# Attention with a wide feed-forward on one core: row maxima of two heads by one instruction, and scores that pass through a double and a single PSUM bank in turn

## The chip, the cores and the metric

The kernel runs on 1 core of one Trainium2 chip. The time is device microseconds of one execution; the figure for a kernel is the median of its runs. PE is TensorE (PEld its weight loads), DVE is VectorE, ACT is ScalarE, POOL is GpSimd, SP is SyncE. PSUM has eight banks here, each 512 float32 wide in 128 partitions, and which of them a step may write is what this case is about.

## The reference

One transformer block on x of 2048 rows by 576 columns: attention of 32 heads of 18 columns each with a full softmax, then a gated feed-forward of width 4608.

```python
x = A_x
h = x + _A_ref(_layernorm(x, axis=-1), A_wqkv, A_wo)
h2 = h + _B_ref(_layernorm(h, axis=-1), B_w_gate, B_w_up, B_w_down)

def _A_ref(x, wqkv, wo):                # H = 32, Dh = 18
    qkv = (lambda x, *d: x.transpose(*d))((x @ wqkv).reshape(B, S, 3, H, Dh), 2, 0, 3, 1, 4)
    q, k, v = qkv[0], qkv[1], qkv[2]
    scores = jnp.einsum("bhqd,bhkd->bhqk", q, k) * Dh ** -0.5
    p = _softmax(scores, axis=-1)
    o = jnp.einsum("bhqk,bhkd->bhqd", p, v)
    return (lambda x, *d: x.transpose(*d))(o, 0, 2, 1, 3).reshape(B, S, D) @ wo

def _B_ref(x, w_gate, w_up, w_down):
    g = jnp.einsum("bsd,df->bsf", x, w_gate)
    u = jnp.einsum("bsd,df->bsf", x, w_up)
    return jnp.einsum("bsf,fd->bsd", _gelu(g) * u, w_down)
```

## The kernel before, in words

Products are made in float16 with each operand split into a high and a low half, so one product of 576 columns is 14 matmuls into one bank (`accumulate`). The program has these stages.

1. Normalization of x, and the products that give q, k and v. The q and k halves go to DRAM (`qk_hi`, `qk_lo`) and come back as stacks of 54 rows for four heads at a time (`load_stacks`); in each stack two heads lie in rows 0 to 53 and 64 to 117.
2. Attention. The work is cut into NS = 32 blocks, indexed n: 8 groups of four heads times 4 blocks of 512 queries. A block has 16 steps, kt, one for each 128 keys. Softmax needs the row maxima first, so the scores are made twice.
   - Maxima (`max_unit`, L420 and L423): queries in the partitions, 512 keys along the row. A unit takes two heads: two matmuls, and the row maximum by DVE. A block has 32 such units, and they run 56 units (28 steps) ahead of the block that uses them. `max_finish` puts the maxima of a block together, PE turns them (L438) and they become two more rows of the q stack.
   - Scores (`scores_pair`, L461 and L463): keys in the partitions, 512 queries along the row, two heads into a double bank, and one Exp by ACT over 1024 elements into `pes`.
   - Weighing (`weigh`, L467): four float32 matmuls of 32 columns each, with v and a column of ones, add one step into the accumulator bank; in the trace they are eight rows.
   - After the 16th step `out_block` copies the accumulator (L476), turns it by four transposes (L480), divides on DVE (L483, L485) and stores on POOL.
   From step 484 on there are no maxima left to make.
3. During the last three blocks of attention, `wo_block` makes the output projection and the second normalization of the query blocks that are done (`fill`), and `split_gate_up` prepares the first feed-forward weights (`side`). The last `wo_block(3)` comes after attention.
4. Feed-forward: nine chunks of 512 columns, `gate_up` and `down`, with the next chunk's weights split beside them. `split_down` first needs the largest weight of the chunk: DVE reduces it (L122, L125), PE turns it (L129).

PE's order in stages 1 to 3 up to the end of attention is the order of the code, since it is scheduled by hand there. After it, and on the other engines, a scheduler decides, within what the buffers allow.

The eight PSUM banks before: two double banks `pair0` and `pair1` (`pair_ring`, for scores; their four halves are `single_ring`, for `gate_up`), and four single banks. The first three are `m_ring`: maxima, the two kinds of transposes, the products of `wo_block`, the small transposes of weights. The fourth, `singles[3]`, is the accumulator. `down` uses the four.

One step of the main loop before is: one unit of maxima, scores of the pair 0, scores of the pair 1, one unit of maxima, weighing of the step before.

## Time and profile before

| What | Value |
|---|---|
| Median of 3 runs | 2922.98 us (2922.92 to 2926.84) |
| The profiled execution | 2924.51 us, of which the span from first to last instruction 2922.7 us |
| PE, DVE, ACT busy over the span | 95%, 68%, 49% |
| Attention, from the first to the last weighing | 228.9 to 1591.2 us |
| Mean granted TensorE clock | 0.997 |

Times in the profile are microseconds from the start of the span. A row of the timeline has the start, the duration, the engine, the line, the operation, out<-in and a count; instructions that follow one another in one engine and line are merged into one row. In brackets stands idle time just before, and what ended it. A mean duration counts an instruction from its start to its end; the next one of the same engine may start before that end, so the distance between two starts is shorter than the duration.

### The profile page before, as it was taken

The numbers are of one execution on the slowest core, as the hardware profiler recorded it, in microseconds if no ns is written. First come the engines' busy times: TensorE is split into PE (matmuls) and PEld (weight loads), VectorE is DVE, ScalarE is ACT, GpSimd is POOL, SyncE is SP. The second block draws the span as 40 slices with busy tenths as digits, with TensorE's granted clock in tenths as the row PEclk, the third lists the DMA queues.
The fourth block names the chain that finished last, engine by engine and source line by source line (L and its number), as shares of the span: only waits on it lengthen the run. The fifth ranks groups of instructions, "written<-read, shape, count | busy, mean of one in ns | idle before, by whom it ended". The sixth has DMA issues, their size and how long they took to land.

```text
span 2922.7 us, 42983 instructions
## 1 busy us (share of the span) xinstructions
PE 2772.1 (95%) x17312; PEld 1168.1 (40%) x17312; DVE 1977.2 (68%) x3675; ACT 1440.0 (49%) x1684; POOL 100.4 (3%) x205
## 2 busy tenths in 40 slices
PE   6999899999999999999989999999999999999999
PEld 3532222222222222222233555555555555555555
DVE  7569999999999999999975725252525252524222
ACT  5217888888888888888757312121212121212111
POOL 0001000100001010100000000000000000000000
PEclk9999999999999999999999999999999999999999
DMA  8121000000000000000225301010101010100001
GB/s 224 51 74 53 1 25 1 26 1 10 17 1 25 1 26 1 25 5 1 58 56 122 105 1 53 1 53 1 53 1 53 1 53 1 53 1 1 1 17 50
DMA packets 105432, 95.13 MB, mean 33 GB/s; under 512 B 65872, under 2 KB 79312, under 8 KB 105232
## 3 DMA queue, kind: packets, MB, share of 16 engines
q1 hardware_dynamic: 100256, 83.81, 10.3%
q0 software_dynamic: 4976, 8.56, 1.0%
q8 instruction: 136, 2.23, 0.3%
q14 instruction: 64, 0.52, 0.1%
HBM read 63.70 MB, written 14.16 MB: 27 GB/s over the span
## 4 chain that ended last, share of the span: by engine, by line
PE 44%; ACT 3%; DVE 2%; DMA 1%; issue 1%; POOL 0%; ACTq 0%; SPq 0%
PE pair L267 27%; PE bank L267 15%; ACT WK L463 1%; DVE mx L423 1%; ACT W L238 1%; ACT V L238 1%; PE bank L467 1%; ACT V L598 0%; DMA X<-nat 0%; PE pair L461 0%; ACT W L598 0%; DMA X<-V 0%; DMA V<-in_B_w_down_dram 0%; ACT ga L613 0%; PE bank L420 0%
## 5 line engine op out<-in xcount | busy, mean ns | idle before, releaser
L423 DVE TENSOR_REDUCE mx<-bank 128x1 f32<-128x512 f32 x2048 | 1282.2, 683 | 61.4 <-PE bank L420 58.8
L463 ACT ACTIVATE WK<-pair,p_ex_sc 128x1024 f32<-128x1024 f32 x1024 | 1085.0, 1113 | 261.9 <-PE pair L461 261.7
L467 PE MATMUL bank<-WK,V 128*32 128x512 f32 x4096 | 548.7, 607 | 0.1
L267 PE MATMUL pair<-X,V 128*128 128x512 f16 x2240 | 489.0, 379 | 3.1 <-ACT ga L613 3.1
L267 PE MATMUL pair<-X,W 128*128 128x512 f16 x2128 | 469.0, 379 | 1.5 <-ACT ga L613 1.5
L615 DVE SCALAR_TENSOR_TENSOR ga<-pair,p_hsc,ga 128x512 f32<-128x512 f32 x144 | 107.8, 749 | 502.5 <-PE pair L267 502.5
L267 PEld LDWEIGHTS <-WK 128*128 128x128 f16 x3456 | 338.2, 98 | 93.2
L613 ACT ACTIVATE ga<-pair,p_gsc 128x512 f32<-128x512 f32 x144 | 98.8, 686 | 491.6 <-PE pair L267 491.6
L420 PE MATMUL bank<-W 54*128 54x512 f16 x1024 | 288.4, 382 | 54.3 <-DVE mx L423 18.1
L267 PEld LDWEIGHTS <-W 128*128 128x128 f16 x2296 | 222.5, 98 | 271.9 <-issue 16.3
L420 PE MATMUL bank<-A 54*128 54x512 f16 x1024 | 279.8, 383 | 46.7 <-DVE mx L423 12.0
L267 PEld LDWEIGHTS <-V 128*128 128x128 f16 x2240 | 218.5, 98 | 261.8 <-issue 3.9
L616 ACT CAST WK<-ga 128x512 f16<-128x512 f32 x144 | 89.0, 618 | 443.6 <-DVE ga L615 443.6
L634 DVE SCALAR_TENSOR_TENSOR nat<-bank,p_dsc,nat 128x288 f32<-128x288 f32 x288 | 148.0, 516 | 194.8 <-PE bank L267 194.8
L467 PEld LDWEIGHTS bank<-WK,V 128*32 128x32 f32 x4096 | 81.2, 108 | 409.2 <-issue 380.5
L267 PE MATMUL bank<-V,WK 128*128 128x288 f16 x1920 | 239.0, 286 | 0.0
L267 PE MATMUL bank<-W,WK 128*128 128x288 f16 x1536 | 191.4, 286 | 0.0
L461 PE MATMUL pair<-W 56*128 56x512 f16 x1024 | 161.1, 378 | 5.6 <-ACT WK L463 5.4
L420 PEld LDWEIGHTS <-W 54*128 54x128 f16 x1024 | 61.6, 93 | 242.2 <-issue 235.2
L461 PE MATMUL pair<-A 56*128 56x512 f16 x1024 | 157.1, 379 | 1.1 <-ACT WK L463 1.1
L420 PEld LDWEIGHTS <-A 54*128 54x128 f16 x1024 | 60.3, 93 | 231.4 <-issue 225.1
L617 DVE TENSOR_TENSOR WK<-ga,WK 128x512 f16<-128x512 f32 x144 | 99.3, 690 | 76.3 <-ACT WK L616 76.2
(154 smaller groups left out, 1140.9 us busy)
## 6 DMA issues: line engine op xcount, KB each, us to landing
V<-in_B_w_down_dram SPq DMA_DIRECT2D x9, 1152.0 KB
A<-in_B_w_gate_dram SPq DMA_DIRECT2D x9, 1024.0 KB
A<-in_B_w_up_dram SPq DMA_DIRECT2D x9, 1024.0 KB
qk_hi<-qk SPq DMA_DIRECT2D x36, 128.0 KB
qk_lo<-qk SPq DMA_DIRECT2D x36, 128.0 KB
A<-in_A_x_dram SPq DMA_DIRECT2D x32, 144.0 KB
out_dram<-nat SPq DMA_DIRECT2D x16, 288.0 KB
WK<-in_A_wqkv_dram SPq DMA_DIRECT2D x3, 1152.0 KB
```

Of the source, the lines that this page charges most:

```text
L238: nc.scalar.activation(wh[:, c], wf[:, c], AF.Copy, scale=sc)
L267: nc.tensor.matmul(dst, a, b, start=(i == 0), stop=(i == len(pairs) - 1))
L420: nc.tensor.matmul(pms[j][:, :TB], Q[r, q0 : q0 + P], K[r, kc * TB : (kc + 1) * TB], start=True, stop=True)
L423: nc.vector.tensor_reduce(mx[:, t, 2 * pr + j, kc : kc + 1], pms[j][:, :TB], axis=AX.X, op=ALU.max)
L461: nc.tensor.matmul(pS[:, j, :TB], K[r, kt * P : (kt + 1) * P], Q[r, qc * TB : (qc + 1) * TB], start=True, stop=True)
L463: nc.scalar.activation(pes[(2 * kt + pr) % NPE], pS[:, :, :TB], AF.Exp, scale=ex_sc)
L467: nc.tensor.matmul(acc[32 * hh : 32 * hh + 32, :TB], Vg[n // NB][:, kt * G4 + hh * VC : kt * G4 + hh * VC + 32], pes[(2 * kt + hh // 2) % ...
L613: nc.scalar.activation(ga, pg[:, :TB], AF.Gelu_apprx_tanh, scale=gsc)
L615: nc.vector.scalar_tensor_tensor(ga, pu[:, :TB], hsc, ga, op0=ALU.mult, op1=ALU.mult)
L616: nc.scalar.copy(hh[:, f], ga)
L617: nc.vector.tensor_sub(hl[:, f], ga, hh[:, f])
L634: nc.vector.scalar_tensor_tensor(nat[:, t, ws], pt[:, :HALF], dsc, nat[:, t, ws], op0=ALU.mult, op1=ALU.add)
```

## The change

PSUM is dealt out anew. Both double banks `max_pairs` now belong to the maxima: a unit's two matmuls go into the two halves of one, and one DVE instruction reduces 128x2x512 to 128x2. The scores have a double bank `sc_pair` and a single bank `sc_one`, and go through them in turn: two heads by an Exp of 1024 elements (`P`), one head by an Exp of 512 elements (`s`). As a step has four heads and P and s together three, the order of the units repeats every three steps. It is written as strings, with A for a unit of maxima and W for the weighing. `pes` has nine slots of one head each. The transposes of the maxima and of `out_block`, the products of `wo_block` and the small transposes of weights now use the halves of `max_pairs`, as `gate_up` does; the products of stage 1 and `down` use the other four banks. `wo_block` is begun at kt 5 instead of kt 1, and its two products in a step stand together behind the weighing.

```diff
-    pairs2 = [ps.tile([P, 2, 512], F32, name=f"pair{i}") for i in range(2)]
-    singles = [ps.tile([P, 512], F32, name=f"bank{i}") for i in range(4)]
+    max_pairs = [ps.tile([P, 2, 512], F32, name=f"pair{i}") for i in range(2)]
+    sc_pair = ps.tile([P, 2, 512], F32, name="scp")
+    sc_one = ps.tile([P, 512], F32, name="sco")
+    acc = ps.tile([P, 512], F32, name="acc")
...
-    pair_ring = ring(pairs2)
-    single_ring = ring([p[:, i] for i in range(2) for p in pairs2])
-    m_ring = ring(singles[:3])
-    down_ring = ring(singles)
+    pair_ring = ring(max_pairs)
+    m_ring = ring([p[:, i] for i in range(2) for p in max_pairs])
+    single_ring = m_ring
+    side_ring = ring([sc_pair[:, 0], sc_one, sc_pair[:, 1], acc])
+    down_ring = side_ring
...
-            pms = [next(m_ring) for j in range(2)]
+            pm = next(pair_ring)
...
-            for j in range(2):
-                nc.vector.tensor_reduce(mx[:, t, 2 * pr + j, kc : kc + 1], pms[j][:, :TB],
-                                        axis=AX.X, op=ALU.max)
+            nc.vector.tensor_reduce(mx[:, t, 2 * pr : 2 * pr + 2, kc], pm[:, :, :TB],
+                                    axis=AX.X, op=ALU.max)
...
+    NPE = 9
...
+    def scores(k):
+        h = done["h"]
+        if h + k > 4 * NS * NT:
+            return
+        done["h"] += k
+        dst = sc_pair if k == 2 else sc_one.unsqueeze(1)
...
+        nc.scalar.activation(pes[:, h % NPE : h % NPE + k], dst[:, :, :TB], AF.Exp, scale=ex_sc)
...
+        order = "APAsW", "PAAsPAsW", "PAsW"
+        for q in range(NS * NT + 1):
+            n, kt = divmod(q, NT)
+            for unit in order[q % 3][:-1]:
+                if unit == "A":
+                    take(mxs)
+                else:
+                    scores(2 if unit == "P" else 1)
+            take(side, 2)
+            if q > 0:
+                weigh(*divmod(q - 1, NT))
...
+            if q > 0:
+                take(fill, 2)
...
+            if n > NS - NB and kt == 5:
+                fill = wo_block(n % NB - 1)
```

How PE's queue changes, at three places. Weight loads and rows that repeat the one above are left out.

The first is a step in the middle of attention. Before, one step (L420 maxima into `bank0` to `bank2`, L461 scores, L467 weighing into `bank3`):

```order
L420 MATMUL bank1_69<-W_75 128x512
L420 MATMUL bank2_70<-W_75 128x512
L461 MATMUL pair0_66<-A_77 128x512
L461 MATMUL pair1_67<-A_77 128x512
L420 MATMUL bank0_68<-W_75 128x512
L420 MATMUL bank1_69<-W_75 128x512
L467 MATMUL bank3_71<-WK_76,V_73 32x512 x4
```

Now, the step of the string PAAsPAsW (L424 maxima, two matmuls to a row, L473 scores, `scp` the double and `sco` the single bank, L479 weighing):

```order
L473 MATMUL scp_68<-A_76 128x512
L424 MATMUL pair0_66<-W_74 128x512
L424 MATMUL pair1_67<-W_74 128x512
L473 MATMUL sco_69<-A_76 128x512
L473 MATMUL scp_68<-A_76 128x512
L424 MATMUL pair0_66<-W_74 128x512
L473 MATMUL sco_69<-A_76 128x512
L479 MATMUL acc_70<-WK_75,V_72 32x512 x4
```

Each head of the maxima had a bank of three in turn; now a unit of two heads has one double bank of two, and the scores one double and one single.

The second is the turning of a finished block, on PE, before (L480):

```order
L420 MATMUL bank0_68<-W_75 128x512
L420 MATMUL bank1_69<-W_75 128x512
L467 MATMUL bank3_71<-WK_76,V_73 32x512 x4
L480 MATMUL bank2_70<-id32_78,WK_76 128x128 x4
L420 MATMUL bank0_68<-W_75 128x512
```

and now (L491):

```order
L424 MATMUL pair1_67<-W_74 128x512
L473 MATMUL sco_69<-A_76 128x512
L479 MATMUL acc_70<-WK_75,V_72 32x512 x4
L491 MATMUL pair1_67<-id32_77,WK_75 128x128 x4
L473 MATMUL scp_68<-A_76 128x512
```

The transposes took the third bank, whose turn it was; now they write into half of the double bank that the unit of maxima just ahead of the weighing has filled.

The third is the end of attention, on PE. Before (X,V are the first products of `gate_up`, W,X the products of `wo_block(3)`, and L129 turns the largest weights: `am_gu` of the second chunk's gate and up, `am_dn` of the first chunk's down):

```order
L480 MATMUL bank0_68<-id32_78,WK_76 128x128 x4
L267 MATMUL pair0_66<-X_74,V_73 128x512
L267 MATMUL pair1_67<-X_74,V_73 128x512
L267 MATMUL bank1_69<-W_75,X_74 128x288
L267 MATMUL bank2_70<-W_75,X_74 128x288
...
L267 MATMUL pair1_67<-X_74,V_73 128x512
L129 MATMUL bank2_70<-id32_78,am_gu_12972 1x128 x2
L267 MATMUL pair0_66<-X_74,V_73 128x512
L129 MATMUL bank0_68<-id32_78,am_dn_12800 1x128
```

and now (L133 and L140 turn and spread the largest weight):

```order
L491 MATMUL pair0_66<-id32_77,WK_75 128x128 x4
L271 MATMUL pair1_67<-W_74,X_73 128x288
L271 MATMUL pair0_66<-W_74,X_73 128x288
...
L133 MATMUL pair1_67<-id32_77,am_dn_12116 1x128
L271 MATMUL pair1_67<-X_73,V_72 128x512
L140 MATMUL pair0_66<-a1_dn_12123,ones_84 128x1
L271 MATMUL pair1_67<-X_73,V_72 128x512
```

Before, 24 products of `gate_up` stood ahead of those of `wo_block(3)` and 110 between these and the turning of `am_dn`; now none stands ahead of them, and none between them and `am_dn`.

More of the change, by code (lines that the diff above doesn't have):

```diff
@@ L329, in v_rows @@
         for i in range(2):
-            pt = next(pair_ring)[:, 0]
+            pt = next(side_ring)
             yield from accumulate(pt[:, :HALF], products(
@@ L416, in max_unit @@
             Q, K = sets[g % 2][pr]
-            pms = [next(m_ring) for j in range(2)]
+            pm = next(pair_ring)
             for j in range(2):
                 r = half(j, R1)
-                nc.tensor.matmul(pms[j][:, :TB], Q[r, q0 : q0 + P],
+                nc.tensor.matmul(pm[:, j, :TB], Q[r, q0 : q0 + P],
                                  K[r, kc * TB : (kc + 1) * TB], start=True, stop=True)
-            for j in range(2):
-                nc.vector.tensor_reduce(mx[:, t, 2 * pr + j, kc : kc + 1], pms[j][:, :TB],
-                                        axis=AX.X, op=ALU.max)
+            nc.vector.tensor_reduce(mx[:, t, 2 * pr : 2 * pr + 2, kc], pm[:, :, :TB],
+                                    axis=AX.X, op=ALU.max)
             yield
@@ L448, in max_finish, with weigh @@
                         "o (t q) -> o t q", q=P), mT[k : k + TPB])
-    NPE = 4
-    pes = [view(WK, 2 * 4 * TB * i, (2, TB)) for i in range(NPE)]
-    oTs = [view(WK, 2 * 4 * TB * NPE + 4 * TB * i, (TB,)) for i in range(2)]
-    def scores_pair(n, kt, pr):
-        g, qc = divmod(n, NB)
-        pS = next(pair_ring)
-        Q, K = sets[g % 2][pr]
-        for j in range(2):
-            r = half(j, R1 + 2)
-            nc.tensor.matmul(pS[:, j, :TB], K[r, kt * P : (kt + 1) * P],
+    NPE = 9
+    pes = view(WK, 0, (NPE, TB))
+    oT = view(WK, 4 * TB * NPE, (TB,))
+    done = {"h": 0}
+    def scores(k):
[4 more added lines that the diff above has]
+        dst = sc_pair if k == 2 else sc_one.unsqueeze(1)
+        for i in range(k):
+            q, hh = divmod(h + i, 4)
+            n, kt = divmod(q, NT)
+            g, qc = divmod(n, NB)
+            Q, K = sets[g % 2][hh // 2]
+            r = half(hh % 2, R1 + 2)
+            nc.tensor.matmul(dst[:, i, :TB], K[r, kt * P : (kt + 1) * P],
                              Q[r, qc * TB : (qc + 1) * TB], start=True, stop=True)
-        nc.scalar.activation(pes[(2 * kt + pr) % NPE], pS[:, :, :TB], AF.Exp, scale=ex_sc)
-    def weigh(n, kt, acc):
+        nc.scalar.activation(pes[:, h % NPE : h % NPE + k], dst[:, :, :TB], AF.Exp, scale=ex_sc)
+    def weigh(n, kt):
         for hh in range(4):
@@ L468, in weigh, with out_block @@
                              Vg[n // NB][:, kt * G4 + hh * VC : kt * G4 + hh * VC + 32],
-                             pes[(2 * kt + hh // 2) % NPE][:, hh % 2],
+                             pes[:, (4 * (n * NT + kt) + hh) % NPE],
                              start=(kt == 0), stop=(kt == NT - 1))
-    def out_block(n, acc):
+    def out_block(n):
         g, qc = divmod(n, NB)
-        oT = oTs[n % 2]
         nc.scalar.copy(oT, acc[:, :TB])
@@ L534, in tile_block @@
     xbs = [view(A, GU + 4 * HALF * i, (HALF,)) for i in range(3)]
-    y = view(WK, 20480, (D,))
+    y = view(WK, 4 * TB * (NPE + 1), (D,))
     ys = [view(V, GU + 4 * FT * D + 2 * L * i, (L,), F16) for i in range(2)]
@@ L642, in qk_block @@
         for j in (0, 4, 5):
-            yield from qk_tile(j, b, next(m_ring))
+            yield from qk_tile(j, b, next(side_ring))
     def v_block(b):
@@ L653, in other_products @@
             for b in range(NB):
-                yield from qk_tile(j, b, next(pair_ring)[:, 0])
+                yield from qk_tile(j, b, next(side_ring))
     kept = []
@@ L674, in tile_block @@
             take(fill, 2 - i % 2)
-        prev = None
-        for n in range(NS):
-            g, qc = divmod(n, NB)
-            acc = singles[3]
-            for kt in range(NT):
-                take(mxs)
-                for pr in range(2):
-                    scores_pair(n, kt, pr)
-                    if g < NG - 1 or kt >= NT // 4:
-                        take(fill)
-                    take(side)
-                take(mxs)
-                if prev is not None:
-                    weigh(*prev)
-                    if prev[0] != n:
-                        ob = out_block(prev[0], prev[2])
-                        next(ob)
-                prev = (n, kt, acc)
-                if n and kt == 1:
-                    take(ob)
-                    if n > NS - NB:
-                        for t in range((qc - 1) * TPB, qc * TPB):
-                            turn(nat16[:, t], t)
-                        run(fill)
-                        fill = wo_block(qc - 1)
-                if g == 0 and qc == 0 and kt == NT - 1:
-                    run(fill)
-                    init_set(sets[1])
-                if g + 1 < NG and kt == 2 and qc == (1 if g == 0 and NB > 1 else 0):
-                    load_stacks(g + 1)
-                if n == min(2, NS - 2) and kt == 2:
-                    side = prepare_wo()
-                if n == NS - NB and kt == 2:
-                    load_gate_up(0)
-                if n == max(NS - 2, NS - NB) and kt == NT * 3 // 4:
-                    run(side)
-                    side = keep(split_gate_up(0))
@@ L712, in tile_block @@
-        weigh(*prev)
-        for _ in out_block(prev[0], prev[2]):
-            pass
+        run(fill)
+        ob = None
+        order = "APAsW", "PAAsPAsW", "PAsW"
+        for q in range(NS * NT + 1):
+            n, kt = divmod(q, NT)
+            for unit in order[q % 3][:-1]:
[6 more added lines that the diff above has]
+                weigh(*divmod(q - 1, NT))
+                if kt == 0:
+                    ob = out_block(n - 1)
+                    next(ob)
+            if n == NS:
+                break
+            if q > 0:
+                take(fill, 2)
+            if n and kt == 1:
+                take(ob)
+                if n > NS - NB:
+                    for t in range((n % NB - 1) * TPB, n % NB * TPB):
+                        turn(nat16[:, t], t)
+                    run(fill)
+            if n > NS - NB and kt == 5:
+                fill = wo_block(n % NB - 1)
+            if n == 0 and kt == 1:
+                init_set(sets[1])
+            if n % NB == (1 if n < NB else 0) and n // NB + 1 < NG and kt == 2:
+                load_stacks(n // NB + 1)
+            if n == 2 and kt == 2:
+                side = prepare_wo()
+            if n == NS - NB and kt == 2:
+                load_gate_up(0)
+            if n == NS - 2 and kt == NT * 3 // 4:
+                run(side)
+                side = keep(split_gate_up(0))
@@ L715, in tile_block @@
+        run(ob)
         run(side)
```

## The prediction

> **What bounds the kernel now.** I read the busy shares by stretches first, then the groups of instructions, then the timeline of single steps. A stretch of stage 1 and one inside attention (columns: PE, PEld, DVE, ACT, POOL busy in us):

> ```profile
> 100.00:200.00 100.00, 100.00 (x563) 46.71 (x562) 69.49 (x112) 20.12 (x85) 0.00 (x0) 1.00 0.13 44
> ...
> 700.00:800.00 100.00, 92.60 (x635) 22.15 (x631) 97.97 (x169) 82.67 (x81) 8.22 (x16) 1.00 0.06 19
> ```

> In attention DVE looks full, 97.97 of 100 us, nearly all of it the row maxima. The durations that the sum needs are in the groups:

> ```profile
> L423 DVE TENSOR_REDUCE mx<-bank 128x1 f32<-128x512 f32 x2048 | 1282.2, 683 | 61.4 <-PE bank L420 58.8
> L463 ACT ACTIVATE WK<-pair,p_ex_sc 128x1024 f32<-128x1024 f32 x1024 | 1085.0, 1113 | 261.9 <-PE pair L461 261.7
> L613 ACT ACTIVATE ga<-pair,p_gsc 128x512 f32<-128x512 f32 x144 | 98.8, 686 | 491.6 <-PE pair L267 491.6
> L476 ACT COPY WK<-bank 128x512 f32<-128x512 f32 x32 | 18.7, 585 | 1.2 <-PE bank L467 1.2
> L122 DVE TENSOR_REDUCE ac_gu<-A 128x1 f32<-128x512 f32 x90 | 56.8, 671 | 0.0
> L122 DVE TENSOR_REDUCE ac_dn<-V 128x1 f32<-128x576 f32 x36 | 25.5, 737 | 2.4 <-DMA V<-in_B_w_down_dram 2.4
> ```

> Then one step in order of time:

> ```profile
> 704.12 1.27 DVE L423 TENSOR_REDUCE mx<-bank 128x1 f32<-128x512 f32 x2
> ...
> 705.43 0.39 PE L420 MATMUL bank<-W 54*128 54x512 f16 x2
> 705.65 0.60 PE L461 MATMUL pair<-A 56*128 56x512 f16 x4
> 705.85 6.83 DVE L423 TENSOR_REDUCE mx<-bank 128x1 f32<-128x512 f32 x11 [0.46 <-PE bank L420]
> 706.09 0.88 PE L420 MATMUL bank<-W 54*128 54x512 f16 x2
> 706.14 2.12 ACT L463 ACTIVATE WK<-pair,p_ex_sc 128x1024 f32<-128x1024 f32 x2 [0.95 <-PE pair L461]
> 706.90 1.06 PE L467 MATMUL bank<-WK,V 128*32 128x512 f32 x8
> 707.90 0.39 PE L420 MATMUL bank<-W 54*128 54x512 f16 x2
> ...
> 709.37 1.07 PE L467 MATMUL bank<-WK,V 128*32 128x512 f32 x8
> ```

> The reader should see that a step takes 709.37 - 706.90 = 2.47 us, while four reduces at their own distance (1.27 - 0.68 = 0.59) need 2.4. What closes the step is a loop through PE: a matmul of maxima to its reduce 0.42 (705.43 to 705.85), the reduce 0.69, 0.05 until the last matmul may write the freed bank (the group at 706.09 ends at 706.97; less the 0.37 of one matmul, its last started at 706.60), 0.30 until the weighing, 1.00 until the next step's first matmul: 2.46. So attention is held by DVE and, nearly as hard, by PE's order; halving DVE's instruction count alone cannot bring the whole fixed part of a reduce.

> **The change, part by part.** New durations, by estimate from these rows. A two-bank reduce: 683 ns plus 512 elements at 66 ns per 64 (576 against 512 in the L122 rows) is 1.21 us, and 0.59 + 0.53 = 1.12 to the next start; above, two single ones, 1.37 and 1.20; below, 1.06, the elements without any fixed part. A single-bank Exp: 0.69, as the other table function from PSUM (L613), between 0.585 (the copy) and 0.71; next start after 0.59. Double Exps start 2.12 - 1.11 = 1.01 apart. A score matmul to its Exp is 0.49 (705.65 to 706.14), group to group on PE 0.22 (705.43 to 705.65).

> *Three steps with maxima.* DVE needs 6 x 1.12 = 6.7 us, ACT 4 x (1.01 + 0.59) = 6.4 against 6.1 before. But P and s have one buffer each, so the next s waits for the Exp of the last s, and everything behind it on PE (the weighing, then the next maxima) waits too. From the first P of PAAsPAsW: 0.49 to its Exp, 1.01 to the Exp of s behind it, 0.69 + 0.05 until the next s may write, 0.30 to W, 1.00; then P, A, s 0.44, W 0.30, 1.00; then A, P, A, s 0.66, W 0.30, 1.00. Sum 7.24 us, or 2.41 to 2.42 a step with rounding: 0.05 less than now, 0.8 in a block of 16 steps. Weighing never waits for its own Exps (they are a step older), and `pes` with nine slots adds no wait, since the slot's last reader stands ahead on PE.

> *Ends of blocks.* A block takes 41.30 us now, 1.8 above 16 steps:

> ```profile
> 698.24 0.21 DVE L430 TENSOR_REDUCE m<-mx 128x16 f32<-128x64 f32 x1
> ...
> 739.54 0.21 DVE L430 TENSOR_REDUCE m<-mx 128x16 f32<-128x64 f32 x1
> ...
> 690.30 1.07 PE L467 MATMUL bank<-WK,V 128*32 128x512 f32 x8
> 691.30 0.66 PE L480 MATMUL bank<-id,WK 128*128 128x128 f32 x4
> ```

> The transposes (L480) start 1.00 behind the weighing, so they wait for no bank. Changed, both transposes of a block (of the maxima and of the output) go into a double bank whose reduce may have just begun: each waits 0 to 1.21, and P, A and ACT behind it. Half of it twice is 1.2; I take 1.1 net. Block: -0.8 + 1.1 = +0.3, over 29 blocks with maxima **+9 us** (with no wait -23, with both whole waits +46).

> *The last 28 steps, without maxima.* Now:

> ```profile
> 1521.32 1.07 PE L467 MATMUL bank<-WK,V 128*32 128x512 f32 x8
> ...
> 1526.61 1.07 PE L467 MATMUL bank<-WK,V 128*32 128x512 f32 x8
> ...
> 1532.60 1.06 PE L467 MATMUL bank<-WK,V 128*32 128x512 f32 x8
> ...
> 1534.61 1.06 PE L467 MATMUL bank<-WK,V 128*32 128x512 f32 x8
> ```

> 2.01 us a bare step, which is two double Exps back to back, and 5.29 with the two products of `wo_block`. Changed, bare PsPsW from its first P at 0: Exp P 0.49, Exp s 1.50; second P (after Exp P) 1.65, its Exp 2.14; second s (after Exp s) 2.24, W 2.54, next P 3.54, second Exp s 3.15 to 3.84, so the next s 3.89, W 4.19, P 5.19; Exp P 4.03, Exp s 5.04 to 5.73, s 5.78, W 6.08, P 7.08. That is 2.36 a step, 0.35 more, on 20 such steps +7. With products, two steps of three cost PE the same 5.3; in the third the second P and s wait 1.8 for Exps while no product can run, on average 0.6 on 8 steps, +5. Together **+12** (0 if products cover it all, +20 if every such step waits).

> *The end of attention.* Here the queue of PE changes most:

> ```profile
> 1592.56 1.04 PE L267 MATMUL pair<-X,V 128*128 128x512 f16 x4
> ...
> 1593.87 4.48 PE L267 MATMUL pair<-X,V 128*128 128x512 f16 x20
> ...
> 1599.58 13.89 PE L267 MATMUL bank<-W,X 128*128 128x288 f16 x112 [1.22 <-DMA X<-nat]
> ...
> 1613.31 12.03 PE L267 MATMUL pair<-X,V 128*128 128x512 f16 x55
> ...
> 1618.40 0.58 DVE L208 TENSOR_SCALAR WK<-nat,rs,nb 128x576 f32<-128x576 f32 x1
> ...
> 1631.18 15.54 SPq L590 DMA_DIRECT2D V<-in_B_w_down_dram  x2
> ...
> 1637.14 2.73 DVE L122 TENSOR_REDUCE ac_dn<-V 128x1 f32<-128x576 f32 x4 [2.44 <-DMA V<-in_B_w_down_dram]
> ...
> 1640.12 0.27 PE L129 MATMUL bank<-id,am_dn 128*1 128x128 f32 x1 [2.69 <-DVE am_dn L125]
> ```

> While POOL and DMA bring the last attention block, PE runs 24 products of `gate_up`, at 0.216 each (4.48 less one of 0.38, over 19) 5.2 us; and between the end of `wo_block(3)` at 1613.3 and the turning of `am_dn` at 1640.1, 110 more, 23.8 us. `am_dn` cannot come sooner: normalization of four row tiles on DVE (from 1618.40), their DMA transposes, then the load of `w_down` into the same region (1631.18 to 1637.14), then 2.73 of reduces. In the changed queue the 24 stand behind `wo_block(3)` and the turning of `am_dn` ahead of nearly all of the 134: PE stands idle until `am_dn` is there. That chain gets some 1.8 us shorter without `gate_up`'s work in between on DVE. 134 x 0.216 - 1.8 = **+27 us** (19 if the chain shortens by 10, 31 if not at all and the spread of the scale, L140, is waited for as well). Everything after it is PE-bound products in the same number, at nothing.

> At nothing too: stage 1's banks (four instead of two or three; PE is 100 us of 100 busy from 100 to 200 us), and the later start of `wo_block`, which gives its DMA transposes four steps more.

> Sum: 9 + 12 + 27 = +48. Against the profiled span of 2922.7 us, whose own execution took 2924.51 (the median of the runs is 2922.98, so the profile adds about 1.5): **2971 us** as a median, slower by 1.6%.

> **The rivals.** (1) Faster: DVE is the bound, and what the reduce saves comes through. For it: 97.97 of 100. Then the step is 6.8/3 = 2.27, -0.20 x 16 + 1.1 = -2.1 a block, -61 + 39 = -22, 2901 us. It needs PE's loop of 7.24 to be 0.44 shorter than its rows; the whole change breaks even at a step of about 2.32. [...] Chance 0.07.
> (2) The idle time at the end of attention isn't paid, because the turning of `am_dn` waits less than its row says, say 1 us: 2971 - 25 = 2946. Against it: PE works its queue in order, and all that L129 waited for stands in the trace. Chance 0.09.
> (3) A reduce over two banks costs two of one bank even in distance, 1.37: 8.2/3 = 2.74 a step, +0.27 x 16 + 1.1 = 5.4 a block, +157 + 39: 3119. Against it: 0.59 apart for 0.68 long, and the slope between the L122 rows. Chance 0.05.
> (4) The losses at blocks and last steps cancel against a better loop, and the end of attention costs less than half: within 0.2%. Chance 0.05.

> **How the numbers follow.** My forecast has 0.74. The range goes down to 2936 (blocks at -23, the rest of the sum +36) and up to 3004 (a reduce distance of 1.20, or both whole waits at most blocks); it holds the forecast but for its tails, and rival 2: about 0.8. Two tenths of a per cent, 6 us, is about what a measurement of this kernel tells from no change. Slower by more: 0.88; within: 0.05; faster: 0.07.

> **What the changed profile would show.** Two-bank reduces of 1.2 us, 1024 of them, with DVE busy below 97 of 100 in attention; weighings in a rhythm of about 1.75, 1.95 and 3.55 us, 7.25 in three; blocks of 41 to 42.5 us; PE waiting for a DVE reduce ahead of L491 and L441; bare last steps at 2.36 instead of 2.01; and one wait of PE on `am_dn` of 23 to 26 us right behind `wo_block(3)`. I am wrong if the rhythm is 6.8 or if that wait is missing.

## The result, and the profile after

The changed kernel takes 3012.69 us (median of 6 runs, 3010.86 to 3020.72), the kernel before 2926.14 on the same chip: a ratio of 1.0303 (95% interval 1.0289 to 1.0317). It is slower, as forecast, but by 87 us instead of 48, above the range. The profiled execution took 3016.96 us, its span 3015.2, which is 92.5 more than the 2922.7 of before. The rows of the matmuls of the weighing cut both spans into four stages:

| Stage | Before, us | After, us | Difference | Forecast |
|---|---|---|---|---|
| start to first weighing | 228.9 | 240.9 | +12.0 | 0 |
| blocks 0 to 28 | 1205.9 | 1233.2 | +27.3 | +9 |
| blocks 29 to 31 | 156.4 | 174.2 | +17.8 | +12 |
| last weighing to end | 1331.5 | 1366.8 | +35.3 | +27 |

The same two stretches as before (PE, PEld, DVE, ACT, POOL busy in us, each with its count of instructions, then the granted clock, the DMA's share and its GB/s):

```profile
100.00:200.00 100.00, 97.06 (x553) 46.94 (x552) 62.21 (x61) 19.73 (x90) 0.00 (x0) 0.98 0.13 43
700.00:800.00 100.00, 89.82 (x616) 20.47 (x613) 90.98 (x90) 85.83 (x105) 9.91 (x19) 0.98 0.07 19
```

DVE is no longer full in attention, 90.98 of 100 against 97.97, and PE does less too; the clock stands at 0.98 instead of 1.00. The new instructions, in the page's groups (busy us, mean ns of one, idle time before them):

```profile
L426 DVE TENSOR_REDUCE mx<-pair 128x2 f32<-128x1024 f32 x1024 | 1200.5, 1219 | 122.3 <-PE pair L424 116.0
L475 ACT ACTIVATE WK<-scp,p_ex_sc 128x1024 f32<-128x1024 f32 x683 | 761.5, 1115 | 212.7 <-PE scp L473 200.0
L475 ACT ACTIVATE WK<-sco,p_ex_sc 128x512 f32<-128x512 f32 x682 | 466.3, 684 | 26.6 <-PE sco L473 25.0
```

The merged reduce takes 1.219 us, the single Exp 0.684: both as estimated (1.21 and 0.69). Three steps with maxima, in the timeline:

```profile
441.66 6.98 DVE L426 TENSOR_REDUCE mx<-pair 128x2 f32<-128x1024 f32 x6 [0.30 <-PE pair L424]
...
442.20 1.07 PE L479 MATMUL acc<-WK,V 128*32 128x512 f32 x8
...
444.07 0.39 PE L424 MATMUL pair<-W 54*128 54x512 f16 x2 [0.27 <-DVE mx L426]
...
444.85 0.39 PE L473 MATMUL scp<-W 56*128 56x512 f16 x2 [0.18 <-ACT WK L475]
...
445.75 1.07 PE L479 MATMUL acc<-WK,V 128*32 128x512 f32 x8
...
447.51 1.06 PE L479 MATMUL acc<-WK,V 128*32 128x512 f32 x8
...
448.94 3.49 DVE L426 TENSOR_REDUCE mx<-pair 128x2 f32<-128x1024 f32 x3 [0.30 <-PE pair L424]
...
449.48 1.07 PE L479 MATMUL acc<-WK,V 128*32 128x512 f32 x8
```

The weighings come 3.55, 1.76 and 1.97 us apart, 7.28 in three; the forecast had 7.24. Six reduces take 6.98, so their starts are (6.98 - 1.22) / 5 = 1.15 apart (the forecast had 1.12), and DVE then waits 0.30. Two short waits of PE (0.27 on a reduce, 0.18 on an Exp) stand beside each other. The end of a block, and the granted clock in four stretches around it:

```profile
550.92 3.49 DVE L426 TENSOR_REDUCE mx<-pair 128x2 f32<-128x1024 f32 x3
...
554.46 0.22 PE L441 MATMUL pair<-id,mm 128*32 128x128 f16 x1 [1.40 <-DVE mx L426]
...
556.51 1.94 PE L479 MATMUL acc<-WK,V 128*32 128x512 f32 x8
...
559.53 1.06 PE L479 MATMUL acc<-WK,V 128*32 128x512 f32 x8
```

```profile
549.00:552.40 3.40, 3.40 (x28) 0.76 (x24) 3.33 (x7) 2.94 (x5) 0.00 (x0) 1.00 0.00 0
552.40:555.83 3.43, 1.85 (x16) 0.52 (x13) 3.01 (x4) 2.18 (x3) 0.00 (x0) 1.00 0.00 0
555.83:559.24 3.41, 3.25 (x14) 0.48 (x13) 1.57 (x2) 1.85 (x4) 0.00 (x0) 0.50 0.03 6
559.24:562.66 3.42, 3.42 (x28) 0.74 (x27) 2.92 (x3) 2.96 (x4) 0.00 (x0) 1.00 0.01 1
```

The transposes of the maxima wait 1.40 us for the reduce that still reads their bank. In that stretch PE works 1.85 of 3.43 us, and in the next 3.41 us its clock is granted at 0.50: the weighing takes 1.94 instead of 1.06. This second price was in no step of the forecast. PE's waits over the whole program (us in total, times, the longest):

```profile
PE pair L424 <- DVE mx L426: 46.0, 133, 2.0
PE scp L473 <- ACT WK L475: 44.1, 137, 1.8
PE pair L441 <- DVE mx L426: 29.1, 30, 2.0
PE pair L133 <- DVE am_dn L129: 25.2, 1, 25.2
...
PE pair L491 <- DVE mx L426: 9.1, 11, 1.5
```

The last steps without maxima and without products:

```profile
1583.46 1.07 PE L479 MATMUL acc<-WK,V 128*32 128x512 f32 x8
1586.99 1.07 PE L479 MATMUL acc<-WK,V 128*32 128x512 f32 x8
1588.65 1.07 PE L479 MATMUL acc<-WK,V 128*32 128x512 f32 x8
1590.53 1.06 PE L479 MATMUL acc<-WK,V 128*32 128x512 f32 x8
```

They take 3.53, 1.66 and 1.88, which is 7.07 in three or 2.36 a step, the forecast number. The end of attention:

```profile
1650.11 0.65 PE L491 MATMUL pair<-id,WK 128*128 128x128 f32 x4 [0.68 <-ACT WK L487]
1656.40 16.49 PE L271 MATMUL pair<-W,X 128*128 128x288 f16 x112 [5.64 <-DMA X<-nat]
1695.11 2.73 DVE L126 TENSOR_REDUCE ac_dn<-V 128x1 f32<-128x576 f32 x4 [8.93 <-DMA V<-in_B_w_down_dram]
1698.09 0.37 PE L133 MATMUL pair<-id,am_dn 128*1 128x128 f32 x1 [25.20 <-DVE am_dn L129]
1699.86 6.31 PE L271 MATMUL pair<-X,V 128*128 128x512 f16 x22
```

PE stands idle for 5.64 and then for 25.20 us, where before it had products of `gate_up`. Behind both waits it runs slower, at half clock by the trace's records (1654.9 to 1661.7 and 1675.4 to 1702.7 us): the 112 products of `wo_block(3)` take 16.49 against 13.89, and 22 products of `gate_up` 6.31 instead of 22 x 0.216 = 4.8. Stage 1 has a wait that was not there before:

```profile
55.53 3.54 PE L271 MATMUL scp<-W,X 128*128 128x288 f16 x14 [4.32 <-DVE qk L326]
```

The first products of v now write banks that the q and k products use, and DVE, busy with normalization (its rows from 49.4 to 54.1 us), empties those late.

The clock's share can be bounded. By the trace's records of the granted clock, the time at half clock was 6.4, 7.3, 3.4 and 0.3 us in the four stages before, and 16.2, 41.9, 17.1 and 34.1 after. If PE loses half of it where it is busy (the weighing at half clock took 1.94 us instead of 1.06), that is at most (109.3 - 17.4) / 2 = 46 us, less some 11 for the 23 us at the end in which PE waited for `am_dn` anyway. That is an estimate of up to some 34 us; between the two profiles the forecast missed 44.

### The profile page after: what moved, and what is told of

The parts are those of the page before. It is cut to its first block, busy times and chain, and to the rows that moved or that the text cites. A ratio compares the mean times of both kernels' runs of the same rounds, so it can differ in the third digit from the quotient of the medians.

```text
span 3015.2 us, 41989 instructions
## 1 busy us (share of the span) xinstructions
PE 2780.2 (92%) x17312; PEld 1154.4 (38%) x17312; DVE 1920.5 (64%) x2651; ACT 1510.6 (50%) x2025; POOL 100.8 (3%) x205
## 4 chain that ended last, share of the span: by engine, by line
PE 67%; ACT 13%; DVE 12%; issue 6%; DMA 2%; SPq 0%; POOL 0%; ACTq 0%; DVEq 0%; POOLq 0%
PE pair L271 29%; PE acc L479 11%; ACT WK L475 10%; DVE mx L426 8%; PE scp L271 7%; PE pair L424 4%; PE scp L473 4%; PE acc L271 3%; PE sco L271 3%; PE sco L473 3%; ACT W L242 1%; ACT V L242 1%; PE pair L491 1%; DVE o L496 0%; ACT W L609 0%
## 5 line engine op out<-in xcount | busy, mean ns | idle before, releaser
L426 DVE TENSOR_REDUCE mx<-pair 128x2 f32<-128x1024 f32 x1024 | 1200.5, 1219 | 122.3 <-PE pair L424 116.0
L475 ACT ACTIVATE WK<-scp,p_ex_sc 128x1024 f32<-128x1024 f32 x683 | 761.5, 1115 | 212.7 <-PE scp L473 200.0
L479 PE MATMUL acc<-WK,V 128*32 128x512 f32 x4096 | 560.3, 619 | 0.3
L475 ACT ACTIVATE WK<-sco,p_ex_sc 128x512 f32<-128x512 f32 x682 | 466.3, 684 | 26.6 <-PE sco L473 25.0
L271 PE MATMUL pair<-X,W 128*128 128x512 f16 x1792 | 390.8, 379 | 1.5 <-ACT ga L624 1.5
L624 ACT ACTIVATE ga<-pair,p_gsc 128x512 f32<-128x512 f32 x144 | 98.8, 686 | 491.7 <-PE pair L271 491.7
L424 PE MATMUL pair<-W 54*128 54x512 f16 x1024 | 201.2, 386 | 38.0 <-DVE mx L426 24.8
L424 PE MATMUL pair<-A 54*128 54x512 f16 x1024 | 200.0, 382 | 31.2 <-DVE mx L426 21.1
L479 PEld LDWEIGHTS acc<-WK,V 128*32 128x32 f32 x4096 | 81.8, 109 | 243.6 <-issue 232.7
L473 PE MATMUL scp<-W 56*128 56x512 f16 x683 | 136.7, 389 | 25.5 <-ACT WK L475 24.8
L473 PE MATMUL scp<-A 56*128 56x512 f16 x683 | 136.2, 387 | 19.9 <-ACT WK L475 19.4
L473 PEld LDWEIGHTS <-A 56*128 56x128 f16 x1024 | 66.8, 94 | 219.3 <-issue 199.5
L473 PEld LDWEIGHTS <-W 56*128 56x128 f16 x1024 | 64.4, 94 | 225.4 <-issue 208.2
L424 PEld LDWEIGHTS <-W 54*128 54x128 f16 x1024 | 66.2, 95 | 188.6 <-issue 168.9
```

The lines of the kernel that those rows point to most:

```text
L271: nc.tensor.matmul(dst, a, b, start=(i == 0), stop=(i == len(pairs) - 1))
L424: nc.tensor.matmul(pm[:, j, :TB], Q[r, q0 : q0 + P], K[r, kc * TB : (kc + 1) * TB], start=True, stop=True)
L426: nc.vector.tensor_reduce(mx[:, t, 2 * pr : 2 * pr + 2, kc], pm[:, :, :TB], axis=AX.X, op=ALU.max)
L473: nc.tensor.matmul(dst[:, i, :TB], K[r, kt * P : (kt + 1) * P], Q[r, qc * TB : (qc + 1) * TB], start=True, stop=True)
L475: nc.scalar.activation(pes[:, h % NPE : h % NPE + k], dst[:, :, :TB], AF.Exp, scale=ex_sc)
L479: nc.tensor.matmul(acc[32 * hh : 32 * hh + 32, :TB], Vg[n // NB][:, kt * G4 + hh * VC : kt * G4 + hh * VC + 32], pes[:, (4 * (n * NT + kt) ...
```

## The experiments

Each stage of loss was taken away by itself (e1 to e3), one was put into the kernel before (e4), then all together, and then the main loop was tested. The kernel before took 2922.83 us beside e1 to e4, 2927.83 beside c1 and the d kernels, 2924.46 beside c2, c3 and f1, and 2924.18 beside g1. So a difference of two kernels that weren't measured together is uncertain by up to some 5 us, and for small gains the stages of the profiles say more than the times.

**e1, the end.** In the changed kernel, all small transposes and `wo_block(3)` go to the other four banks once attention is over:

```diff
+    small_ring = [m_ring]          # wo_block and the small transposes take next(small_ring[0])
...
     e, gsc, hsc = kept[0]
+    small_ring[0] = side_ring
```

> The changed kernel, with one thing put back: after attention the products of wo_block(3) and the small transposes of weights take banks that gate_up doesn't use. Theory A (PE's queue at the end of attention): gate_up's first products stand ahead of wo_block(3) again, PE's wait of 25.2 us on am_dn and the half clock behind it go, the stretch from the last weighing to the end falls from 1366.9 us to about 1332, and the time by 33 to 35 us, to about 2978. Rival B (the wait on am_dn only covers work that DVE and DMA have to do anyhow, so another wait takes its place): under 10 us.

Measured: 2988.05 us (ratio 1.0226, 1.0208 to 1.0243), 24.6 less than the changed kernel. The end takes 1339.9 us instead of 1366.8. PE's rows there:

```profile
1670.99 14.84 PE L273 MATMUL pair<-X,V 128*128 128x512 f16 x68
1685.66 0.38 PE L135 MATMUL scp<-id,am_gu 128*1 128x128 f32 x2
...
1698.26 0.37 PE L135 MATMUL scp<-id,am_dn 128*1 128x128 f32 x1 [5.75 <-DVE am_dn L131]
```

`gate_up` again runs while `am_dn` is awaited, and the wait falls from 25.20 to 5.75. Counted from the last weighing, `am_dn` is turned after 52.3 us here and after 49.7 in the changed kernel: PE's work in between lengthens the chain that makes it by 2.6 us at most. So the queue position of its turning was the cause. Of the end 8.4 us remain against before: the chain is 3.4 us longer than the 48.9 of before, 126 products stand ahead of `am_dn` instead of 134, and the clock is at one half for 4.4 us behind the wait.

**e4, the same into the kernel before.** `wo_block(3)` and the small transposes after attention go to the halves of the scores' double banks there, and nothing else changes:

```diff
+    small_ring[0] = single_ring    # in the kernel before, after attention
```

> The kernel before, with only the end of attention as in the change: the products of wo_block(3) and the small transposes of weights share gate_up's banks from there on. Theory A: PE waits about 25 us on am_dn, part of what follows runs at half clock, and the time rises by 31 to 36 us, to about 2959. Rival B (the wait hurts only together with the changed attention): under 10 us.

Measured: 2954.57 us (ratio 1.0106, 1.0091 to 1.0121), 31.7 more, with the end at 1361.1 us and the same wait:

```profile
1642.56 0.37 PE L131 MATMUL pair<-id,am_dn 128*1 128x128 f32 x1 [24.95 <-DVE am_dn L127]
```

Sharing the banks of `gate_up` at this one place lengthens the end of the kernel before by 29.6 us, most of the 35.3 that the end costs the changed one. So this loss is not a matter of the merged instruction or of the scores.

**e2, stage 1.** The first block of v products takes the halves of the maxima's banks:

```diff
-                run(v_block(0))
+                run(v_block(0, m_ring))    # v_rows takes next(ring) instead of next(side_ring)
```

> The changed kernel, with the first v products in the banks of the maxima, which nothing else uses then, so that they don't wait for DVE to empty the banks of the q and k products. Theory A (shared banks in stage 1): PE's wait of 4.3 us at 51 us and the half clock behind it go, the first maxima come at about 96 us instead of 102.1, the time falls by 6 to 8 us. Rival B (the clock at the start is low for other reasons, and the later start of maxima is made up by attention anyway): under 2 us.

Measured: 3006.87 us (1.0288, 1.0273 to 1.0304), 5.8 less by the medians and 2.5 less when each is taken against the kernel before beside it. So the time alone doesn't show a gain; the stage does. The first weighing comes at 232.3 us instead of 240.9; in the seven profiles with this edit it comes at 230.5 to 236.9, in the four of the changed kernel without it (`e1`, `e3` and `f1` among them) at 236.2 to 240.9, a mean difference of 6.0. The wait of 4.32 us is gone:

```profile
50.83 3.59 PE L271 MATMUL pair<-W,X 128*128 128x288 f16 x28
```

**e3, the two transposes of a block.** They take a whole turn in the ring of double banks, hence the pair that was reduced longest ago, instead of half of the next:

```diff
-        pt = next(m_ring)                   # both in max_finish and in out_block
+        pt = next(pair_ring)[:, 0]
```

> The changed kernel, with the two transposes of each block put into the double bank whose turn it is (the one that was reduced longest ago) instead of a half that the last unit of maxima has just filled. Theory A (transposes wait for a reduce, and the idle PE then loses half its clock): waits of PE ahead of L441 and L491 fall from 29 and 9 us in sum to under 6, blocks take 40.5 to 41.5 us instead of 40.8 to 42.6, most of the half-clock windows inside attention go, and the time falls by 20 to 35 us. Rival B (the step's own loop with one double and one single bank sets the block, and the transposes only fill its idle time): under 5 us. Rival C (the clock falls because PE is less dense in the new step order, whatever the transposes do): blocks of 40.5 to 41.5 but as many half-clock windows as now, -15 us.

Measured: 2983.14 us (1.0201, 1.0186 to 1.0217), 29.5 less. Blocks 0 to 28 take 1202.7 us, 3.2 less than before the change. PE's waits over the whole program:

```profile
PE pair L424 <- DVE mx L426: 70.9, 171, 1.7
PE pair L441 <- DVE mx L426: 3.0, 11, 0.4
...
PE pair L491 <- DVE mx L426: 0.7, 1, 0.7
```

The 29.1 us ahead of L441 and the 9.1 ahead of L491 shrink to 3.0 and 0.7, and 25 us more of waiting turn up at the maxima, in waits of 0.41 us on average where those ahead of L441 had 0.97. Time at half clock in these blocks falls from 41.9 to 11.3 us. As the order repeats every three steps and a block has 16, there are three kinds of blocks. Those in which the clock stays full take 41.64, 40.84 and 42.62 us in turn in the changed kernel, and 40.71, 40.61 and 41.63 here: 0.72 less on average, 21 us in 29 blocks. The other 9.7 of the 30.5 us lie in blocks in which the clock fell. There are 30.6 us less at half clock, of which by the estimate above up to half is time lost, so the clock can account for them.

**c1, all three.**

> The changed kernel with the three edits e1, e2 and e3 together (banks at the end, in stage 1 and for the transposes). If the losses are separate, each at its own place, their gains add up: 24.6 + 5.8 + 29.5 = 60 us less than the changed kernel's 3012.7, so 2953, and what is left against the kernel before (30 us) lies in the last 28 steps (some 15), the rest of the end (8), stage 1 (3.4). If a single cause (the halved clock, say, that one disturbance sets off and the next prolongs) lay behind several of them, the sum would not be reached or be overshot by more than 8 us.

Measured: 2951.38 us (1.0079, 1.0061 to 1.0097), 61.3 less than the changed kernel, where the single gains add up to 59.9. Taken against the kernel before beside each, they are 63.0 and 50.0, so the times alone don't settle the sum. The stages agree better: in c1 the end is 28 us shorter than in the changed kernel (27 in e1), blocks 0 to 28 are 29.5 shorter (30.5 in e3), and the first weighing comes 4.0 sooner (8.6 in e2). So the losses at the end and in the blocks are separate.

**c2, the last 28 steps as well.** Where no maxima are left, the scores go through two double banks as before:

```diff
+            while q >= 484 and done["h"] < min(4 * q + 4, 4 * NS * NT):
+                ...                         # k = 2, or 1 where pes or the heads end
+                b = next(ring of sc_pair and max_pairs[0])
+                scores(k, b if k == 2 else b[:, :1])
```

> The three edits together, and in the last 28 steps, which have no maxima, the scores go through two double banks in turn as in the kernel before (the second is the first bank pair of the maxima; transposes and the other products take the single bank and the second pair). If the last steps lose time because P and s have one buffer each, they come back to what they took before: 173.7 us fall to some 157, so 2951.4 - 16 = 2935. If they lose it because the order of the products of the last blocks is another, under 6 us.

Measured: 2937.42 us (1.0047, 1.0032 to 1.0062), 14.0 less than c1. Blocks 29 to 31 fall from 173.7 to 164.7 us, so 9 of the expected 16 came; as c1 stands at half clock for 13.7 us more in these blocks, how much of the 9 is the clock's isn't shown. Most of the rest of the difference lies ahead of the first weighing (236.9 against 231.2), where the code is the same and c1 had 6 us more at half clock. Against before there remain 8.3 us in these blocks, 5.5 at the end and 2.3 ahead of the first weighing, against a gain of 3.7 in blocks 0 to 28.

**d1, d2, d3: what sets the pace of the main loop.** On top of c1, once each. d1 leaves half of the keys out of the maxima, d2 half of the queries out of the single Exps, and d3 does both, so they serve for the time alone:

```diff
-            nc.vector.tensor_reduce(..., pm[:, :, :TB], ...)               # d1, d3
+            nc.vector.tensor_reduce(..., pm[:, :, : TB // 2], ...)
-        nc.scalar.activation(pes[...], dst[:, :, :TB], AF.Exp, ...)        # d2, d3, for k == 1
+        nc.scalar.activation(pes[..., :m], dst[:, :, :m], AF.Exp, ...)     # m = TB // 2
```

> On top of the three edits, each row maximum is taken over half of the columns (the other half of the keys is left out of the maxima): DVE's 1024 two-bank reduces become some 0.53 us shorter, nothing else changes. If DVE sets the pace of attention, three steps fall from 7.28 us to PE's own work of some 6.7, so 80 us or more in all. By the forecast's chain through P, s and PE, which no reduce is part of, nothing (within 5 us). If several loops of about the same length hold each other (P and its Exp, s and its Exp, the reduce and its bank), 0.03 us in three steps, 5 us in all.

> On top of the three edits, the Exp of a single bank runs over half of its columns (the weights of the other half of the queries are left as they were): ACT's 700 or so single Exps become some 0.21 us shorter. By the forecast's chain, which has one single Exp of 0.69 in three steps, 0.21 us in three, 35 us in all. If several loops of about the same length hold each other, 0.03 us in three steps, 5 us in all. If DVE sets the pace, nothing.

> d1 and d2 together. Several loops: more than the sum of both, 0.165 us in three steps, some 27 us in all. The forecast's single chain: the same 35 us as d2. DVE: the same as d1, 80 us or more.

Measured, one run each: 2907.73, 2943.54 and 2880.40 us, which is 44, 8 and 71 less than c1; the 8 lie within the spread of c1's own four runs (2945.10 to 2954.62). The median of three steps goes from 7.28 to 7.25, 7.25 and 7.11 us. DVE over 900 us of attention, c1 first, then d1 (columns as in the stretches above):

```profile
500.00:1400.00 900.00, 818.18 (x5708) 190.34 (x5706) 842.89 (x833) 795.01 (x955) 54.99 (x105) 1.00 0.05 14
```

```profile
500.00:1400.00 900.00, 812.98 (x5827) 194.75 (x5826) 507.12 (x859) 811.61 (x977) 55.93 (x106) 1.00 0.05 14
```

With 336 us of DVE's work gone from these 900, three steady steps are only 0.03 us faster: DVE alone doesn't set their pace. Nor does the forecast's chain through P and s, since taking 0.21 from its single Exp gave 0.03 of it; only both together give 0.17. This is what the expectations gave for several loops of nearly the same length that hold each other (0.03, 0.03 and 0.165), of which the forecast's chain is one. But none of the three expectations had d1's 44 us, of which the steady steps bring 5. The three kinds of blocks in turn go from 40.71, 40.61 and 41.63 to 39.47, 39.93 and 41.15 us, 0.80 less on average and 23 us in 29 blocks, of which 5 are the steady steps' and 18 come at the ends of blocks; 5.2 us are ahead of the first weighing, where c1 and c2 differ as much with the same code, and 10.5 in the last blocks. With shorter waits there was also less half clock, 17 us up to the last weighing against 44. A likely reason, taken up by c3, is that DVE has other work at the end of a block, and with six reduces in 6.98 of 7.28 us catches up slowly.

**f1, the merged instruction undone by itself.** The changed kernel, with two single-bank reduces on the same double bank:

```diff
-            nc.vector.tensor_reduce(mx[:, t, 2 * pr : 2 * pr + 2, kc], pm[:, :, :TB], axis=AX.X, op=ALU.max)
+            for j in range(2):
+                nc.vector.tensor_reduce(mx[:, t, 2 * pr + j, kc : kc + 1], pm[:, j, :TB], axis=AX.X, op=ALU.max)
```

> The changed kernel, with the maxima of a double bank taken by two single-bank instructions again (their banks, the order of the scores and all else as changed): what the merged instruction brings by itself. DVE's distance for two heads goes from 1.13 to about 1.19. By the forecast's chain through P, s and PE, which holds no reduce, steady steps stay at 7.28 us in three and only the ends of blocks and the first maxima suffer: under 15 us slower than the changed kernel. If DVE is in fact full there (its groups of six reduces leave 0.3 us of 7.28), its six pairs need 7.14 us and the 1.9 us of other work in a block cannot be caught up: 1 to 2 us a block, 30 to 60 us slower.

Measured: 3035.67 us (1.0379, 1.0362 to 1.0396), 23 more than the changed kernel, between the two expectations. Its steady three steps:

```profile
446.87 7.27 DVE L427 TENSOR_REDUCE mx<-pair 128x1 f32<-128x512 f32 x12 [0.17 <-PE pair L424]
```

Twelve reduces in 7.27 are (7.27 - 0.68) / 11 = 0.60 apart, 1.20 for two, against 1.15: the merge saves 0.046 us of DVE (before rounding) an instruction, 47 us in 1024, and half of it arrives. With two reduces the three steps take 7.43, of which DVE waits 0.17, so there it comes close to setting the pace. The merged instruction by itself is a gain of 23 us, so the rest of the change, the banks dealt out anew and the order that follows from them, costs 87 + 23 = 110 us.

**c3 and g1, DVE's other work.** The halves of the maxima are made on POOL, in c2 and in the kernel before:

```diff
-        nc.vector.tensor_scalar_mul(mm[:, :, 0], m, 1 / MSC)
-        nc.vector.scalar_tensor_tensor(mm[:, :, 1], m, 1 / MSC, mm[:, :, 0], op0=ALU.mult, op1=ALU.subtract)
+        nc.gpsimd.tensor_scalar_mul(ms, m, 1 / MSC)
+        nc.gpsimd.tensor_copy(mm[:, :, 0], ms)
+        nc.gpsimd.tensor_sub(mm[:, :, 1], ms, mm[:, :, 0])
```

> As c2_tail, and the two small DVE instructions that make the halves of the maxima (0.17 us each, once a block) go to GpSimd as three. Halving the reduces shortened a block by 0.9 us at its end and the steady steps by 0.03 in three: so DVE's other work at the end of a block is what the reduces cannot catch up. By that, 0.3 us a block comes back, 9 us less than c2_tail over 29 blocks. If instead the transposes' waits alone make the block's end, nothing (within 3 us), or a loss if GpSimd's results come late for them.

> The kernel before, with the halves of the maxima made on GpSimd as in c3_pool (three small instructions there, two of 0.16 us fewer on DVE in each block). In the kernel before DVE stands at 97.97 of 100 us in attention and a block takes 1.8 us more than 16 steps. If DVE's other work in a block is what makes up the end of a block there, it gets 0.32 us shorter in each of 29 blocks: 9 us less, 2914. If the loop through PE sets the pace (2.46 of 2.47 us a step) and the transposes the block's end, nothing (within 3 us).

Measured: c3 2935.30 us (1.0037, 1.0024 to 1.0050), which can't be told from c2; blocks at full clock of 40.36, 40.62 and 41.49 us are 0.16 shorter on average, but blocks 0 to 28 stood at half clock for 6 us more. g1 2920.37 us (0.9989, 0.9980 to 0.9998): of the kernels with the whole computation the only one below the one before, by 0.1%, less than its expectation of 9 us. A block there takes 41.12 instead of 41.30, so 0.18 of the 0.32 us taken from DVE come through. So DVE's other work is one part of what makes the end of a block: in both kernels about half of what was taken from DVE comes through.

## Why the prediction was wrong in size

**Right.** The sign, the durations of the new instructions, the rhythm (7.24 forecast, 7.28 measured), bare last steps at 2.36, the wait of PE on `am_dn` (23 to 26 forecast, 25.20 measured), the transposes' waits (half of 1.21 twice a block, 1.2; measured 38.2 us in 32 blocks, also 1.2, but as 30 waits of 0.97 at L441 and 11 of 0.83 at L491). Blocks at full clock average 41.70 us, 0.40 above the 41.30 of before: 12 us in 29 blocks, against the forecast 9.

**Wrong: a wait costs only its own length.** The forecast priced each wait at its length. The halved clock behind it was left out. It is seen in the rows (a weighing of 1.94 us instead of 1.06, the products of `wo_block(3)` in 16.49 instead of 13.89); its sum, up to some 34 us, is an estimate from the clock records. In blocks 0 to 28, 12 of the 27.3 us are in the blocks at full clock and the other 15 come with the blocks at half clock (41.9 us there against 7.3 before); when e3 took the waits away, the half clock fell too, to 11.3 us. In the last steps (17.8 instead of 12) there are 17.1 us at half clock against 3.4, which can account for the miss; no run separates it from the scores' buffers.

**Wrong: the end at 134 x 0.216 - 1.8 = 27.** All 134 products did fall behind `am_dn`, but the end grew by 35.3 us. The part of the chain behind `wo_block(3)` did get shorter, from 26.7 us (1613.5 to 1640.1) to 25.2 (1672.9 to 1698.1). Ahead of it the products of `wo_block(3)` lost 2.6 us at half clock, for which the forecast had no term, so from the last weighing to the turning of `am_dn` it is 48.9 us before (1591.2 to 1640.1) and 49.7 after (1648.4 to 1698.1). The other 34.5 us of the loss come behind the turning: 29 for the 134 products, some 2 for those that run at half clock for the first 4.6 us. The last 3 or so are not accounted for.

**Wrong: "at nothing too: stage 1's banks".** The reason given was PE at 100 of 100 busy from 100 to 200 us. The loss lies ahead of that, at 51 to 61 us, where DVE is the busy engine (9.90 of 10 us, against 5.68 of PE) and, as the reader of the shared banks, is late. The number of banks in the ring grew, as the forecast said; who empties them had to be asked. The stage lost 12.0 us: the wait of 4.32, and 9.8 us more at half clock, of which by the same estimate up to half is time lost.

**Right number, incomplete reason: the loop.** The forecast derived 7.24 from one chain, and by it d2 would have taken 0.21 us out of three steps; it took 0.03. The chain holds no reduce, so by it f1 would have stayed at 7.28; it took 7.43. With d3 this shows several loops, so that the number fitted was in part luck.

**The rivals.** Rival 1 (2901, DVE the bound) fails on d1 for steady steps, though DVE's share at the ends of blocks is real; the 1024 instructions fewer are worth 47 us of DVE time by f1, of which 23 reach the end. Rival 2 (idle end not paid) fails on e1 and e4. Rival 3 (a reduce at 1.37) fails on 1.15, and rival 4 (within 0.2%) on 3.0%.

**What stays open.** The 12 us between c2 and the kernel before, of which 8.3 lie in the last three blocks; some 3 us at the end; and how the clock's share divides among single waits: no kernel held the waits and changed the clock alone, because no PSUM bank was free for work that would fill them.

## What to carry to other kernels

When an edit takes PSUM banks from other users, price every user that now shares a bank, by who empties it and when: here the merged instruction gained 23 us, and its banks, taken from the transposes, the end, stage 1 and the last steps, cost 110. Here PE ran its matmuls in the order of its queue (it stood idle for 25.20 us ahead of `am_dn`, with products of `gate_up` behind it that in e1 ran meanwhile), so one late reader became a wait for everything behind it; giving the waiting matmul another bank (e1, e2, e3) took back 60 us without touching the order of the steps. A chain through the trace that adds up to the period isn't proof that its links set it: shorten a link before paying for it.

## What the runs showed of the hardware

| PE idle in a stretch of 3.41 us | Stretches | Next at half clock |
|---|---|---|
| under 1.0 us | 5466 | 1 |
| 1.0 to 1.4 us | 241 | 24 |
| 1.4 to 1.8 us | 72 | 43 |
| over 1.8 us | 36 | 36 |

Over 1.8 us of idle time in such a stretch was followed by half clock every time, 36 of 36, and 1.4 to 1.8 us 43 times of 72. So the wait of 1.40 us at the end of a block cost up to 1.7 us more in the next stretch, by an estimate of half of 3.41, as the clock stood at 0.50 there.
